# Segment 0 loads its successor's left rows through an idle buffer, turns the second left values ahead of the softmax weights, and the MLP's first loads come in another order

## The chip, the cores and the metric

One core of one Trainium2 chip. The metric is the device time of one execution in microseconds (us). A core has a matrix engine (TensorE, "PE" in the profile, with its weight loads as "PEld"), a vector engine (VectorE, "DVE"), a scalar engine (ScalarE, "ACT"), a general one (GpSimd, "POOL") and a sequencer for transfers (SyncE, "SP"). Loads and stores are issued on the queues of SP, ScalarE or GpSimd, and the same DMA engines carry them out.

## The reference

The output is `x + A(layernorm(x)) + B(layernorm(x))` for 2048 rows of 1024 bf16 numbers. B is an MLP with a hidden width of 3584. A is attention with a recurrent memory: the rows come in 64 segments of 32, and the first 8 output rows of a segment are the memory of the next.

```python
xn = _layernorm(x, axis=-1)
return x + _A_ref(xn, ...) + _B_ref(xn, ...)

# A, for each of 64 segments
h = concatenate([mem, xs])          # 8 + 32 rows
q, k, v = h @ Wq, h @ Wk, h @ Wv    # 32 heads of 128
p = softmax(where(mask, q @ k.T * scale, -1e9))
o = (p @ v) @ Wo
mem = o[:8]; outs.append(o[8:])

# B
h = gelu(x @ w1 + b1)
return h @ w2 + b2
```

## The kernel before

The program has two stages. The first is the MLP, with the layer norm (profile: up to about 401 us). The second goes through the 64 segments one after the other, since each needs the memory of the one before it.

**The MLP's start.** `load_x` (L386) brings tiles of 128 rows of x, `load_w1` (L397) a pair of column blocks of `w1`, all on SP's queue, in the order x0, x1, w1 pair 0, x2, x3, w1 pair 1, `b1rows` (L404), w1 pairs 2 to 5. While the first x is on its way, TensorE does `WARM` = 13 products on the identity (`idle_products`, L563). Then for each x tile: VectorE's statistics (L438, L440), ScalarE's square root (L447), VectorE's reciprocal and normalization (L453, L457), eight transposes on TensorE (L466), and ScalarE copies the result out (L471). Between the tiles TensorE begins the first MLP products: `begin(tt, pair)` multiplies x tile `tt` with w1 pair `pair` (two groups of eight products, L550). `BEGIN_AT` says which of them run after which transposes. VectorE does these steps in the order written, so the first statistics of tile 2 (`ln_half(tt + 2, 0)` at the end of the turn of tile 0) stand ahead of the normalization of tile 1.

**A segment.** 24 of its 32 rows and the 8 memory rows are the 32 columns of `hT`, its main rows. The other 8 rows of four segments in a row are put together, 32 columns again, as the group's left rows, `hrL` (`hL` in the code). `renew_left` (L317) copies a part of them into `hrL` from a buffer that `load_left_rows` (L313) has filled. The weights are 64 units of 512 KB: for K, Q and V two half-passes of eight units each, in the order K0, Q0, K1, Q1, V0, V1, and 16 units for O. 47 units stay in the core's memory. 17 are streamed anew for each segment, into a ring of six places (L299, SP's queue); two of these come from copies kept in PSUM (L284, VectorE). A place takes its next load when the product that used it is done (`unit_done`).

`half_pass` goes through the eight units of a half-pass: products with the main rows (L856, `hr_home`) and, where the group needs them, with the left rows (L856, `hrL`). Segment 0 does all six half-passes for the left rows of group 0, three units behind the main ones. Functions placed in `at` run between the units: `scores`, `exps`, `sums` and `values` are the attention steps. `sums(u)` makes the softmax denominators, and at its end the weights `pd` (L1024 and L1028 on VectorE). `values(u, ...)` multiplies them with the values: L1043 for the main rows, L1049 for the left rows. The left values of a half-pass, `VL[u]`, are copied out of PSUM (L914) into a staging buffer and turned by `by_slot` with two transposes on VectorE (L920, L921). In segment 0 the staging buffer of V1 is `hr_home`, the 512 columns of both `homes`.

`homes[0]` and `homes[1]` are the two halves of `hr_home`. `homes[s % 2]` holds the main rows of segment s; `load_x_rows(s + 1)` (L309) fills the other one with the next segment's rows, and L1191 then loads the residual into the one that is free again. In the first seven segments these loads are issued by ScalarE (`loads`), and `renew_left` runs on VectorE (`mover`).

After V1 come the O units (L1093). Unit 5 is followed by `values(1, ...)`. Ahead of unit 12 `fold` (L1108 on ScalarE, L1109 and L1110 on VectorE) and at the end L1227 put the four blocks of the sums together. Then, at the end of segment 0:

```python
lead_products(LEAD_FIRST)                        # 16 products on hrL, for segment 1's V0
put_mem(o_sb, nxt["hT"], mixed[:, 224:288], ...) # L344 on TensorE, L354 on VectorE, into homes[1]
lead_products(LEAD)                              # 8 more
```

and segment 1's products on `hr_home` begin. In the kernel before, the left rows of group 1 for two segments are loaded at O unit 6 of segment 0, into `pd_main`, and copied at once:

```python
if n == 6 and first:
    load_left_rows(1, 0, 2, pd_main[:, 0:128], loads)
    renew_left(pd_main[:, 0:128], 0, 2, mover)
```

The order on each engine and queue is the order in which the program writes the instructions; no planner moves them.

Of the kernel before, what the change touches and what calls it, by code (L numbers as in the profile page):

```python
# [17 lines left out]
P = 128  # L18
# [45 lines left out]
LATER = 4  # L64
LAG = 3
STREAM_BUFS = 6
WARM = 13
FILL = 4
LATE_FROM = 5
BEGIN_AT = ((), (), ((0, 1), (1, 1)), ((2, 1),))  # L70
BEGUN = 4
NPAIR = 12
MAIN_FIRST = True
# [54 lines left out]
def kernel(  # L128
# [16 lines left out]
    nc = tc.nc  # L145
# [163 lines left out]
        eng.dma_start(out=homes[s % 2], in_=rows_d[s, :, :])  # L309
        nxt["hT"] = homes[s % 2].rearrange("p (k t) -> p k t", k=KT)  # L310

    def load_left_rows(g, s0, s1, out, eng=nc.sync):
        eng.dma_start(out=out, in_=rowsL_d[g, :, 64 * s0:64 * s1])  # L313

    def renew_left(rows, s0, s1, eng):

# [56 lines left out]
    with tc.tile_pool(name="ma", bufs=2) as ma:  # L373
# [7 lines left out]
        def load_x(tt):  # L381
            k = tt // 2 % 4
            if tt % 2 == 0:
                pairs_of_x[k] = slab(f"xt{k}")
            xt = pairs_of_x[k][:, DM * (tt % 2):DM * (tt % 2) + DM]
            nc.sync.dma_start(out=xt, in_=x_flat[tt * P:(tt + 1) * P, :])  # L386
            return xt

        xtoks = {tt: load_x(tt) for tt in range(2)}
        o_sb = nat_home  # L390
        nc.vector.memset(o_sb[:, 0:8, :], 0.0)
        w1_sb, w2_sb = [], []
# [6 lines left out]

        b1rows = ma.tile([FC, P], BF16, name="b1rows", bufs=1)  # L400
        load_w1(range(1))
        xtoks.update({tt: load_x(tt) for tt in range(2, 4)})
        load_w1(range(1, 2))
        nc.sync.dma_start(out=b1rows[:, :], in_=B_b1.rearrange("(fc p) -> fc p", p=P))  # L404
        load_w1(range(2, 6))
        masks_out()
        for j in range(4):
# [153 lines left out]
        def idle_products(n):  # L561
            for _ in range(n):
                nc.tensor.matmul(  # L563
                    idle.rearrange("p (a b) -> p a b", b=P), lhsT=ident, rhs=ident[:, None, :].to_broadcast([P, 4, P]),
                    start=True, stop=True,
                )

        def begin(tt, pair):
            for k0 in range(0, KT, 4):
                for fb in (2 * pair, 2 * pair + 1):  # L570
                    first_product(begun[fb], fb, xnT, 4 * tt, 4 * tt + 4, range(k0, k0 + 4))
# [5 lines left out]
        for tt in range(4):  # L577
            ln_rstd(tt, tt + 1)
            pT = turned(ln_apply(tt))
            for t, pair in BEGIN_AT[tt]:  # L580
                begin(t, pair)
            if tt == 0:
                idle_products(FILL)
            if tt < 3:
                ln_half(tt + 1, 1)
            turned_out(tt, pT, 0, xnT, nc.scalar.copy if tt < 3 else nc.vector.tensor_copy)
            if tt < 3:
                ln_sqrt(tt + 1, tt + 2)
            turned_out(tt, pT, 1, xnT, nc.scalar.copy)
            begin(tt, 0)  # L590
            if tt < 2:
                ln_half(tt + 2, 0)
# [10 lines left out]
        for tg in range(4):  # L603
# [19 lines left out]
            for fb in range(FC):  # L623
                if tg == 0 and fb < BEGUN:
                    ps = begun[fb]
# [129 lines left out]
    with tc.tile_pool(name="late", bufs=1) as late:  # L755
# [70 lines left out]
        for s in range(NSEG):  # L826
# [103 lines left out]
            def turn_k(ps, u):  # L930
                st["kT", u] = nat_home
                turn(ps, nat_home, nc.scalar.copy)
# [64 lines left out]
            def sums(u):  # L997
                prA, prB = st["pr", u]
                dA = mixed[:, 0:160].rearrange("p (c q) -> p c q", q=40)
                for j in range(4):  # L1000
                    q = slice(32 * j, 32 * j + 32)
                    nc.tensor.matmul(
                        dA[q, :, :], lhsT=bd[:, j:j + 1].to_broadcast([P, 32]), rhs=prA, start=True, stop=False,
                        skip_group_check=True, tile_position=(0, 32 * j),
                    )
                for j in range(4):
                    q = slice(32 * j, 32 * j + 32)
                    nc.tensor.matmul(
                        ends(dA[q, :, :]), lhsT=bd[:, j:j + 1].to_broadcast([P, 32]),
                        rhs=prB,  # L1010
                        start=False, stop=True, skip_group_check=True, tile_position=(0, 32 * j),
                    )
                nc.scalar.activation(out=mixed[:, 0:160], in_=mixed[:, 0:160], func=ACT.Ln)  # L1013

                for b in (1, 0):
                    nc.scalar.activation(  # L1016
                        out=mixed[:, 160 * b:160 * b + 160], in_=mixed[:, 0:160], func=ACT.Exp, scale=-1.0,
                        bias=off[:, b:b + 1],
                    )
                pdA = pd_main.rearrange("p (c b q) -> p c b q", c=4, b=2)  # L1020
                place = qL_slots[0] if first or VALUES_0[i4][0] < VALUES_0[i4][1] else ko_slots[0]
                pdB = q_all[:, 512:640] if u else place[:, :, i4]
                dd = mixed[:, 0:320].rearrange("p (b c q) -> p b c q", b=2, q=40)
                nc.vector.tensor_tensor(  # L1024
                    out=pdA.rearrange("p c b q -> p b c q"), in0=prA[:, None, :, :].to_broadcast([P, 2, 4, 40]),
                    in1=dd, op=ALU.mult,
                )
                nc.vector.tensor_tensor(  # L1028
                    out=pdB.rearrange("p (c b a q) -> p b c a q", c=4, b=2, q=NL),
                    in0=prB[:, None, :, :, :].to_broadcast([P, 2, 4, 2, NL]),  # L1030
                    in1=dd.rearrange("p b c (e q) -> p b c e q", q=NL)[:, :, :, ::4, :], op=ALU.mult,
                )
                st["pd", u] = pdA, pdB
# [90 lines left out]
                lambda ps: turn_kL(ps, 0),  # L1124
            )
            turn_k(psK, 0)

            def first_queries(ps):

# [30 lines left out]

            def staged(u):

                return lambda ps: values_out(ps, (VL[1] if u == 0 else hr_home) if first else qL_flat[u], nc.vector.tensor_copy if u == 0 else nc.scalar.copy)

            psV, psVL = half_pass("V", 0, left_v[0], {}, staged(0))
            if first:
# [16 lines left out]

            psV1, psV1L = half_pass("V", 1, left_v[1], at)
            st["V", 1] = values_out(psV1, v_home, nc.scalar.copy)
            if left_v[1]:
                staged(1)(psV1L)
            if first:
                by_slot(1, hr_home)
                load_x_rows(s + 1, loads)  # L1190
            loads.dma_start(out=homes[s % 2], in_=res_d[s + 1, :, :])  # L1191
            if i4 == 1 and more:
# [7 lines left out]
            for n, unit in enumerate(O_UNITS):  # L1200
                t = unit_tile(unit)
                if n == NPAIR and not left_o:
                    st["folded"] = fold(psX)
                    psX = new_acc()
                o_product(n, t, psX)
                unit_done(unit)
                for fn in at.get(n, ()):
                    fn()
                if n == 6 and first:
                    load_left_rows(1, 0, 2, pd_main[:, 0:128], loads)  # L1210
                    renew_left(pd_main[:, 0:128], 0, 2, mover)
                if n == 6 and left_o:
                    st["resL"] = pd_main[:, 0:256]
                    loads.dma_start(
                        out=st["resL"], in_=resL_d[g, :, :]
                    )
# [91 lines left out]
```

## Time and profile before

| | |
|---|---|
| median of 3 runs | 1748.77 us (1744.26 to 1749.96) |
| the profiled execution | 1745.82 us, its span 1744.1 us |
| TensorE busy | 97% of the span |
| VectorE, ScalarE, GpSimd busy | 60%, 40%, 16% |
| MLP, about | 0 to 401 us |
| segment 0, about | 401 to 437 us |
| a later segment, about | 20.8 us ((1740 - 431) / 63) |
| read from HBM, written | 558.98 MB, 26.54 MB |

How to read it: times in a row are microseconds from the start of the span. A row of the order in time has start, length, engine, line, operation, output and inputs, and how many instructions were merged; in brackets stands the idle time ahead of it and what ended it. `ACTq` and `SPq` are the issues of transfers by ScalarE and SP; a transfer lands later than its issue ends. A row of the waits has the waiting engine and line, what it waited for, the sum, the number of times and the longest. A row of a stretch has its bounds, its length, the busy time of PE, PEld, DVE, ACT and POOL (with instructions), the clock that TensorE was granted (1.00 is full), the share of time that the DMA engines were busy, and GB/s. The DMA share can pass 1, since packets overlap.

### The profile page before, as it was taken

The page shows a single profiled execution, that of the slowest core. Times are in us where ns is not written, and L with a number is a line of the kernel's source. Part 1 is how long each engine was busy: PE and PEld are TensorE (multiplying, and loading weights), DVE is VectorE, ACT ScalarE, POOL GpSimd, SP SyncE. Part 2 cuts the span into 40 slices and gives each one's busy share as a digit, 9 for nine tenths or more (in the row PEclk, how much of TensorE's full clock was granted, in tenths as well). Part 3 has the DMA queues.
Part 4 walks back from the last instruction along what each step waited for, and adds up shares of the span by engine and source line. Part 5 has one row for each costly group of instructions (what it writes and reads, how often), then busy time and mean ns, then how long its engine had stood idle before and what let it go on. Part 6 is the DMA issues. An engine that isn't in the chain of part 4 may idle for free. (4 is left out here: it accounts for less than half of the span.)

```text
span 1744.1 us, 66334 instructions
## 1 busy us (share of the span) xinstructions
PE 1688.5 (97%) x28348; PEld 835.4 (48%) x28368; DVE 1040.6 (60%) x2656; ACT 702.5 (40%) x1743; POOL 287.2 (16%) x575
## 2 busy tenths in 40 slices
PE   9999999998999999999999999999999999999998
PEld 5444444444444444544444544444444444444444
DVE  7648383844555565656565565656565656565655
ACT  6335160612333334444443344444434444344433
POOL 0000001412210112121211121111212121212111
PEclk9999999999999999999999999999999999999999
DMA  9446321879999999999999999999999999999998
GB/s 278 155 147 190 84 56 41 269 257 355 336 374 376 369 391 370 399 385 397 376 401 379 394 383 389 391 380 398 380 401 382 395 375 386 367 396 382 398 382 323
DMA packets 236635, 579.36 MB, mean 332 GB/s; under 512 B 63747, under 2 KB 92611, under 8 KB 236340
## 3 DMA queue, kind: packets, MB, share of 16 engines
q1 hardware_dynamic: 204120, 555.50, 84.8%
q0 software_dynamic: 15680, 14.35, 2.5%
q10 hardware_dynamic: 16540, 5.28, 1.2%
q8 instruction: 222, 3.64, 0.8%
q14 instruction: 73, 0.60, 0.1%
HBM read 558.98 MB, written 26.54 MB: 336 GB/s over the span
## 5 line engine op out<-in xcount | busy, mean ns | idle before, releaser
L856 PE MATMUL acc<-u,hr_home 128*32 128x512 bf16 x11456 | 760.9, 380 | 13.5 <-DMA u<-Wc_V 5.3
L856 PEld LDWEIGHTS <-hr_home 128*32 128x32 bf16 x12288 | 333.9, 97 | 313.3 <-issue 40.7
L856 PE MATMUL acc<-u,hrL 128*32 128x512 bf16 x2991 | 259.4, 382 | 5.8 <-DVE hrL L317 5.6
L550 PE MATMUL ps<-u 128*128 128x512 bf16 (+1 forms) x992 | 195.4, 358 | 0.8 <-ACT u L471 0.7
L910 ACT CAST d_oL<-acc 128x512 bf16<-128x512 f32 x143 | 82.8, 583 | 253.0 <-PE acc L856 197.9
L284 DVE TENSOR_SCALAR u<-kept 128x512 uint32<-128x512 uint32 x254 | 162.0, 679 | 30.0 <-PE acc L856 21.7
L1093 PE MATMUL acc<-u,d_oL 128*32 128x512 bf16 x2560 | 162.1, 380 | 1.8 <-DMA u<-Wc_O 1.6
L1093 PE MATMUL acc<-u,kq 128*32 128x256 bf16 (+1 forms) x2688 | 137.9, 319 | 12.5 <-DMA u<-Wc_O 10.6
L681 PE MATMUL ps<-u 128*128 128x512 bf16 x657 | 145.2, 379 | 0.8
L550 PEld LDWEIGHTS <-u 128*128 128x128 bf16 x992 | 91.8, 98 | 102.9 <-issue 1.1
L1093 PEld LDWEIGHTS <-kq 128*32 128x32 bf16 x3328 | 86.9, 96 | 92.3 <-issue 23.7
L1024 DVE TENSOR_TENSOR pd_main<-kq,mixed 128x320 bf16<-128x320 bf16 x128 | 62.4, 488 | 112.0 <-ACT mixed L1016 110.1
L1270 POOL DMA_DIRECT2D out_dram<-hr_home x168 | 85.0, 512 | 251.0 <-DVE hr_home L1246 250.6
L940 ACT CAST kq<-acc 128x256 bf16<-128x256 f32 x256 | 88.9, 375 | 89.2 <-PE acc L856 52.5
L993 DVE TENSOR_TENSOR kq<-kq,mixed 128x96 bf16<-128x96 bf16 x128 | 26.1, 204 | 163.0 <-ACT kq L986 84.0
L856 PEld LDWEIGHTS <-hrL 128*32 128x32 bf16 x3200 | 85.7, 97 | 58.2 <-issue 6.4
L944 DVE STREAM_TRANSPOSE kq<-kq 128x256 bf16<-128x256 bf16 x256 | 98.0, 421 | 16.9 <-ACT kq L940 16.8
L914 ACT CAST kq<-acc 128x512 bf16<-128x512 f32 x128 | 75.1, 587 | 80.0 <-PE mixed L975 77.7
L681 PEld LDWEIGHTS <-u 128*128 128x128 bf16 x672 | 65.6, 98 | 78.8 <-DVE u L638 0.4
L630 ACT ACTIVATE u<-ps,b1col 128x512 bf16<-128x512 f32 x112 | 76.5, 684 | 66.2 <-PE ps L550 64.2
L1016 ACT ACTIVATE mixed<-mixed,small_consts 128x160 f32<-128x160 f32 x256 | 94.3, 368 | 8.4
L1093 PEld LDWEIGHTS <-d_oL 128*32 128x32 bf16 x2560 | 65.1, 96 | 57.1 <-issue 3.0
(142 smaller groups left out, 1912.7 us busy)
## 6 DMA issues: line engine op xcount, KB each, us to landing
u<-Wc_K SPq DMA_DIRECT2D x256, 512.0 KB
u<-Wc_O SPq DMA_DIRECT2D x256, 512.0 KB
u<-Wc_Q SPq DMA_DIRECT2D x192, 512.0 KB
u<-Wc_V SPq DMA_DIRECT2D x192, 512.0 KB
u<-Wc_V SPq DMA_DIRECT2D x63, 320.0 KB
u<-in_B_w_dram SPq DMA_DIRECT2D x28, 512.0 KB
u<-in_A_Wq_dram SPq DMA_DIRECT2D x13, 512.0 KB
u<-in_A_Wv_dram SPq DMA_DIRECT2D x12, 512.0 KB
```

The source lines that it names most:

```text
L284: nc.vector.tensor_single_scalar(out=out, in_=in_, scalar=0, op=ALU.bitwise_or)
L550: nc.tensor.matmul(ps[:, SEG * s0:SEG * s1].rearrange("p (s t) -> p s t", t=SEG), lhsT=w1_sb[fb // 2][:, kt, (fb % 2) * P:(fb % 2 + 1) * P ...
L630: nc.scalar.activation(out=xb[:, :], in_=ps[:, :], func=ACT.Identity, bias=b1col[:, fb:fb + 1], scale=1.0)
L681: nc.tensor.matmul(ps[:, :], lhsT=gts[fc // 4][:, fc % 4, t * P:(t + 1) * P], rhs=w2_sb[fc // 2][:, fc % 2, cs], start=(fc == 0), stop=(fc ...
L856: nc.tensor.matmul(o, lhsT=lhs[:, i, :], rhs=m, start=(i == seq[0]), stop=(i == seq[-1]), tile_position=(0, 32 * j),)
L910: cp(out=out, in_=ps.rearrange("p (h e) -> p h e", e=32))
L914: cp(out=t[:, :], in_=ps[:, :])
L940: nc.scalar.copy(out=q_home[:, h0:h1, NL:40], in_=ps[:, 32 * h0:32 * h1].rearrange("p (h e) -> p h e", e=32))
L944: nc.vector.transpose(out=half, in_=half)
L1016: nc.scalar.activation(out=mixed[:, 160 * b:160 * b + 160], in_=mixed[:, 0:160], func=ACT.Exp, scale=-1.0, bias=off[:, b:b + 1],)
L1093: nc.tensor.matmul(acc[r0:r0 + rows, 0:256 * len(blocks)], lhsT=lhsT, skip_group_check=True, rhs=o_columns(t, k, blocks), start=start, sto ...
L1270: loads.dma_start(out=out_flat[rows, 256 * j:256 * j + 256], in_=res[32 * j:32 * j + NX, :])
```

## The change

1. The left rows of group 1 for two segments are loaded right after K0 of segment 0, by SP, into `homes[1]`, which holds nothing between the MLP and segment 1's rows. They are copied into `hrL` right after V1, ahead of the copy of the second left values.
2. In segment 0 the second left values are copied out by VectorE, no longer by ScalarE, and turned before the weights of the second half are made: these are split from `sums` as `weights(u)`, and in segment 0 `weights(1)` follows `by_slot(1, ...)`.
3. At the MLP's start x2 is loaded ahead of w1 pair 0, `b1rows` goes to ScalarE's queue, `WARM` is 12, and `begin(tt - 1, 1)` runs after the transposes of each tile from the second on.

```diff
-WARM = 13
+WARM = 12
-BEGIN_AT = ((), (), ((0, 1), (1, 1)), ((2, 1),))
...
-    def load_left_rows(g, s0, s1, out, eng=nc.sync):
-        eng.dma_start(out=out, in_=rowsL_d[g, :, 64 * s0:64 * s1])
+    def load_left_rows(g, s0, s1, out):
+        nc.sync.dma_start(out=out, in_=rowsL_d[g, :, 64 * s0:64 * s1])
...
-        xtoks = {tt: load_x(tt) for tt in range(2)}
+        xtoks = {tt: load_x(tt) for tt in range(3)}
...
         load_w1(range(1))
-        xtoks.update({tt: load_x(tt) for tt in range(2, 4)})
+        xtoks[3] = load_x(3)
         load_w1(range(1, 2))
-        nc.sync.dma_start(out=b1rows[:, :], in_=B_b1.rearrange("(fc p) -> fc p", p=P))
+        nc.scalar.dma_start(out=b1rows[:, :], in_=B_b1.rearrange("(fc p) -> fc p", p=P))
...
             pT = turned(ln_apply(tt))
-            for t, pair in BEGIN_AT[tt]:
-                begin(t, pair)
             if tt == 0:
                 idle_products(FILL)
+            else:
+                begin(tt - 1, 1)
...
+                if not (first and u):
+                    weights(u)
+
+            def weights(u):
+                prA, prB = st["pr", u]
                 pdA = pd_main.rearrange("p (c b q) -> p c b q", c=4, b=2)
...
             turn_k(psK, 0)
+            if first:
+                load_left_rows(1, 0, 2, homes[1][:, 0:128])
...
-                return lambda ps: values_out(ps, (VL[1] if u == 0 else hr_home) if first else qL_flat[u], nc.vector.tensor_copy if u == 0 else nc.scalar.copy)
+                return lambda ps: values_out(ps, (VL[1] if u == 0 else hr_home) if first else qL_flat[u], nc.vector.tensor_copy if first or u == 0 else nc.scalar.copy)
...
             st["V", 1] = values_out(psV1, v_home, nc.scalar.copy)
+            if first:
+                renew_left(homes[1][:, 0:128], 0, 2, mover)
             if left_v[1]:
                 staged(1)(psV1L)
             if first:
                 by_slot(1, hr_home)
+                weights(1)
                 load_x_rows(s + 1, loads)
...
-                if n == 6 and first:
-                    load_left_rows(1, 0, 2, pd_main[:, 0:128], loads)
-                    renew_left(pd_main[:, 0:128], 0, 2, mover)
```

## The prediction

> **What bounds the kernel now.** The page was read first, then the list of waits, then the place of the longest TensorE wait in order of time, and last the same place by stretches.
>
> ```profile
> span 1744.1 us, 66334 instructions
> PE 1688.5 (97%) x28348; PEld 835.4 (48%) x28368; DVE 1040.6 (60%) x2656; ACT 702.5 (40%) x1743; POOL 287.2 (16%) x575
> ...
> DVE hrL L317 <- DMA pd_main<-rowsL_d: 6.6, 1, 6.6
> PE acc L856 <- DVE hrL L317: 5.6, 1, 5.6
> PE acc L1093 <- DMA u<-Wc_O: 12.1, 29, 1.0
> ```
>
> TensorE is busy for 97% of the span, so a change gains where TensorE stands still. Its longest single wait stands in the rows of L317: at the end of segment 0 it waits 5.6 us for `hrL`, which VectorE can't write until 32 KB of left rows have landed. The last row is the other limit: from 440 us on, TensorE waits 29 times for a streamed weight, in all 12.1 us.
>
> In order of time (columns: start, length, engine, line, operation):
>
> ```profile
> 423.81 0.84 PE L856 MATMUL acc<-u,hrL 128*32 128x512 bf16 x12
> 425.89 0.64 PE L1043 MATMUL acc<-pd_main,kq 64*128 64x80 bf16 x8
> 427.73 0.23 PE L1049 MATMUL acc<-kq,VL 64*128 64x128 bf16 x2 [1.20 <-DVE VL L921]
> 429.03 0.61 PE L1093 MATMUL acc<-u,kq 128*32 128x512 bf16 x8 [0.53 <-ACT kq L1062]
> 429.90 1.17 PE L1093 MATMUL acc<-u,kq 128*32 128x256 bf16 x32
> 436.64 1.90 PE L856 MATMUL acc<-u,hrL 128*32 128x512 bf16 x16 [5.57 <-DVE hrL L317]
> 439.47 0.64 PE L856 MATMUL acc<-low,hr_home 128*32 128x512 bf16 x4
> 440.72 0.38 PE L856 MATMUL acc<-u,hr_home 128*32 128x512 bf16 x4
> ...
> 419.91 0.69 DVE L914 CAST VL<-acc 128x512 bf16<-128x512 f32 x1 [1.19 <-PE acc L856]
> 423.80 0.63 DVE L1062 CAST d_oL<-acc 128x256 bf16<-128x256 f32 x2 [1.06 <-PE acc L1049]
> 425.22 0.49 DVE L1024 TENSOR_TENSOR pd_main<-kq,mixed 128x320 bf16<-128x320 bf16 x1 [0.80 <-ACT mixed L1016]
> 425.75 0.29 DVE L1028 TENSOR_TENSOR kq<-kq,mixed 128x128 bf16<-128x128 bf16 x1
> 426.96 0.71 DVE L921 STREAM_TRANSPOSE VL<-hr_home 128x512 bf16<-128x512 bf16 x1
> 436.36 0.23 DVE L317 COPY hrL<-pd_main 128x128 bf16<-128x128 bf16 x1 [6.58 <-DMA pd_main<-rowsL_d]
> 438.75 0.23 DVE L354 CAST hr_home<-mixed 128x64 bf16<-128x64 f32 x1 [0.72 <-PE mixed L344]
> ...
> 425.59 0.59 ACT L914 CAST hr_home<-acc 128x512 bf16<-128x512 f32 x1
> 427.75 0.33 ACTq L309 DMA_DIRECT2D hr_home<-rows_d  x1
> 428.12 0.45 ACTq L1191 DMA_DIRECT2D hr_home<-res_d  x1
> 428.61 0.37 ACT L1062 CAST kq<-acc 128x256 bf16<-128x256 f32 x1 [2.42 <-PE acc L1093]
> 428.71 0.34 ACTq L313 DMA_DIRECT2D pd_main<-rowsL_d  x1
> ```
>
> The O products end at 429.90 + 1.17 = 431.07; the next product starts at 436.64. The load was issued at 428.71 and used at 436.36, 7.65 us later. After the wait TensorE is slow as well: the 16 products on `hrL` take 1.90, though 12 took 0.84 before it. The same place by stretches (length, TensorE busy, ..., granted clock, DMA share, GB/s):
>
> ```profile
> 431.00:436.60 5.60, 0.08 (x4) 0.00 (x0) 0.23 (x1) 0.00 (x0) 1.65 (x3) 0.75 1.03 396
> 436.60:442.00 5.40, 5.36 (x62) 1.97 (x66) 2.53 (x7) 0.00 (x0) 1.65 (x3) 0.62 0.28 75
> 442.00:446.00 4.00, 4.00 (x96) 2.03 (x92) 2.43 (x8) 1.80 (x5) 2.18 (x4) 1.00 0.82 288
> 446.00:476.00 30.00, 28.73 (x590) 14.73 (x582) 18.23 (x49) 13.96 (x39) 7.17 (x13) 1.00 1.02 380
> ```
>
> TensorE's stop also stops the DMA engines, a little later: they are full until 436.6, then at 0.28 and 0.82, because the weight places stay occupied, and full again (1.02) from 446.
>
> **Part by part.** *The left rows' load* (`load_left_rows(1, 0, 2, ...)`) goes from ScalarE's queue, after O unit 6, to SP's queue right after the first K half-pass, at about 407 us, into `homes[1]`. Even at its 7.65 us it lands by 415; `hrL` may be overwritten only when its last product of segment 0 ends, 423.81 + 0.84 = 424.65. It has some 10 us of cover. On SP it takes about 0.35 us (the 0.34 of L313), and as the program's eight completion semaphores of the load queues go round, the next loads of V wait for one load later than they did. Their cover is a full DMA queue; the price is 0, and 0.35 us of DMA at the most if it is gone.
>
> *`renew_left`* now runs behind the V products: VectorE 0.23 at 424.70. *The second left values* are copied by VectorE instead of ScalarE (0.69, by the L914 row of 419.91, for 0.59) and turned before the weights: copy 424.97 to 425.66, two transposes of 0.71 to 427.15 (before: 426.96 + 0.71 = 427.67). Then the weights: L1024 to 427.68, L1028 to 428.0 (before: 426.04). So TensorE's L1043 starts at 427.75 for 425.89 and, with 0.64 and 0.23, the values end near 428.6 for 427.96: 0.65 us worse. Behind it waits ScalarE's L1062, which before was held until 428.61 by the issue of two loads (427.75 and 428.12). These now go out at 427.25, so ScalarE is free at 428.1 and L1062 follows the values at 428.65. The O products go on at about 429.1 for 429.03. I take 0 to 0.1, between 0 and 0.65; all of it lies ahead of the wait that comes next.
>
> *What is late next.* With `hrL` ready, its first 16 products (0.84 for 12 and 0.23 more, so 1.1) run from 431.1 to 432.2. The memory rows are put (L344) near 432.1, and VectorE's L354 then writes into `homes[1]`, into which segment 1's rows must have landed. When do they? SP's queue tells it:
>
> ```profile
> 431.61 9.30 SPq L299 DMA_DIRECT2D u<-Wc_Q  x2
> ...
> SPq L299 <- DMA hr_home<-rows_d: 1.4, 1, 1.4
> ...
> q1 hardware_dynamic: 408, 1.42, 101.2%
> ...
> q10 hardware_dynamic: 365, 0.14, 21.1%
> ```
>
> SP issued one load at 431.61 (some 0.3 of issue) and then waited 1.4 us for the rows' semaphore: they landed near 433.3, 5.5 us after issue. The row of q1, SP's queue, is from the queues of 427.5 to 431, where ScalarE's queue, q10, has no row: it has not moved one packet, and moves 365 in the next stretch, 431 to 433.5. It stood behind weights issued earlier. Issued 0.5 us sooner, behind the same weights, the rows land between 432.8 and 433.3; I take 433.2, as nothing is issued in those 0.5 us. L354 then ends near 433.45, and the first product on `hr_home` starts at 433.5: a new wait of about 0.9 us, too short to lower the clock (the 1.20 us before 427.73 did not: eight products in 0.61 at 429.03).
>
> [...]
>
> *TensorE's gain.* The fourth group on `hr_home`, the first at full speed, starts at 440.72; after the change at 433.5 + 3 x 0.23 = 434.2 (a group of four takes 0.38 and three groups 0.84, so (0.84 - 0.38) / 2 = 0.23 from start to start). That is 6.5 us.
>
> *The DMA's gain* is smaller, and it is what counts: in the stretch 446 to 476 the queue is full (1.02) while TensorE stands still for 1.3 us, so the weights, not TensorE, end each of the next segments. What the queue lost is 5.4 x (1.03 - 0.28) / 1.03 = 3.9 plus 4.0 x (1.03 - 0.82) / 1.03 = 0.8, together 4.7 us by shares; by bytes, 5.4 x (396 - 75) / 396 + 4.0 x (396 - 288) / 396 = 5.5. I take 5.2, nearer the bytes, since small packets raise the share; ends 4.7 and 6.5.
>
> *The MLP's start.*
>
> ```profile
> 1.43 5.73 PE L563 MATMUL ps<-hr_home 128*128 128x512 bf16 x13 [1.43 <-POOL hr_home masks.py:199]
> 8.38 1.25 PE L550 MATMUL ps<-u 128*128 128x128 bf16 x16
> 10.22 0.62 PE L466 MATMUL pT<-hr_home,u 128*128 128x128 bf16 x8 [0.59 <-DVE u L457]
> 11.52 1.27 PE L550 MATMUL ps<-u 128*128 128x128 bf16 x16 [0.67 <-ACT u L471]
> ...
> 8.82 0.69 DVE L438 BATCH_NORM_STATS2 ln_stats<-u 128x6 f32<-128x512 bf16 x1 [1.68 <-DMA u<-in_A_x_dram]
> ...
> DMA packets 1401, 1.30 MB, mean 194 GB/s; under 512 B 57, under 2 KB 1005, under 8 KB 1401
> ...
> DMA packets 2585, 2.06 MB, mean 231 GB/s; under 512 B 114, under 2 KB 2073, under 8 KB 2585
> ```
>
> One idle product less is 0.43 (5.73 over 13 and a tail), and the third x tile ahead of the first weights frees VectorE's 1.68 us wait, so the second transposes (10.22) could start 0.4 to 1 us sooner. Against this, the first weights move back by 256 KB (0.7 us at about 350 GB/s): the products at 8.38 start between 7.95 and 8.9. Then `begin(0, 1)` now stands ahead of `begin(1, 0)` and needs the second weights, which keep their place in the queue: packets 128 x 4 + 1024 x 2 = 2560. The packet counts are those up to 6.7 and to 8.9 us. Packet 1408, the end of the third tile, passed at 6.7, and VectorE had the tile at 8.82, a lag of 2.1; packet 2560 passed by 8.9, so the second weights land near 11.1. From there the same seven groups of products and two transposes remain as from 11.52 before. I take -0.3 us; ends -1.9 (no wait, 9.6) and +0.7 (the weights later by the first ones' 0.7). `b1rows` on ScalarE's queue costs one issue (some 0.4 us) ahead of the first table load, which is wanted long after; 0.
>
> *Sum:* -5.2 - 0.3 = -5.5 us, from 1745.82 (1.7 more than its span) to 1740.3. The profiled execution is 3.0 under the median of the runs (1748.77), the four executions' middle is 1747.3; on that level the forecast is 1741.8.
>
> **The rivals.** (B) The whole stall goes: the rows land before L354 (the other queue's packets let by), and segment 1 has slack in its streams. L354 then ends near 432.6, the fourth group on `hr_home` starts at 432.65 + 0.69 = 433.35, and TensorE gains 440.72 - 433.35 = 7.4, with the MLP 7.7: 1739.6. For it: TensorE's own gain is above the DMA's; against it: the DMA share of 1.02. (C) Only part is kept: the queue's 3.9 us, and the second weights land 0.7 late: -3.2, 1744.1. For it: the share is already 1.03 when TensorE would go on. (D) Slower: TensorE now enters segment 1 with its weights just landing, and each of the 63 segments ends in a short wait for `Wc_O`; it would need 5.5 / 63 = 0.09 us a segment more than today to cancel the gain, and 0.17 to be 0.3% slower: 1752.5. For it: 29 such waits stand there already. Against it: the order of instructions from segment 1 on is the same. (E) The change doesn't do what it says: the left rows land after 431, on SP behind weights; 16 us at 7.65 us a load exclude it nearly.
>
> **How the numbers follow.** 0.3% is 5.2 us, about what a measurement of this kernel can tell from no change. Chances: forecast 0.55, B 0.20, C 0.16, D 0.07, E 0.02. The forecast's own range is 5.0 to 6.8 with the MLP (1740.5 to 1742.3), three quarters of it over 5.2; with B that makes 0.62 faster. The last quarter, C and E are 0.31 within. D is slower. The range of 1738 to 1747 leaves out D and the tails: it takes in B and C and the 1.5 us by which runs stand off their middle.
>
> **What would show it.** Right: no wait for `hrL` in the list; a wait of 0.5 to 1.2 us at L354 for `rows_d`; the granted clock full from 424 to 450; DMA share above 1 all through; the first product on `hr_home` near 433.2 (433.5 less the MLP's 0.3); one wait for the second weights near 11 us. Wrong: TensorE waiting over 2 us at segment 1's V or O products, which would be C, or the rows landing before 432, which is B, or the waits for `Wc_O` after 500 us well over today's, which is D.

## The result and the profile after

The changed kernel takes 1740.31 us (median of 17 runs, 1734.42 to 1744.04), the kernel before 1747.30 (17 runs): a ratio of 0.9958, with a 95% interval of 0.9945 to 0.9970. By that ratio it is 7.3 us less, between 5.2 and 9.6. The profiled execution took 1743.2 us with a span of 1741.5; it lies on the upper side of its runs, while that of before lay on the lower side, so the two spans differ by only 2.6 us. The places compared below are near the start of the attention stage. Segment 0 does not start at the same time in every run, so the table below counts them from its start, the first product on `hr_home`.

TensorE's waits of the changed kernel between 420 and 480 us:

```profile
PE acc L1097 <- DMA u<-Wc_O: 2.8, 4, 1.3
PE acc L1047 <- DVE pd_main L1028: 1.6, 1, 1.6
PE acc L855 <- DMA u<-Wc_V: 1.2, 1, 1.2
```

The wait for `hrL`, 5.6 us before, is gone. In its place stand waits for streamed weights (`Wc_O`, `Wc_V`), and one for the weights of the second half (`pd_main`), which are now made later. The changed kernel in order of time (L855 answers to L856 of before, L1097 to L1093, L1047 to L1043, L353 to L354):

```profile
400.92 0.40 PE L855 MATMUL acc<-u,hr_home 128*32 128x512 bf16 x4
427.16 0.32 PE L1047 MATMUL acc<-pd_main,kq 64*128 64x80 bf16 x8 [1.61 <-DVE pd_main L1028]
430.33 0.84 PE L1097 MATMUL acc<-u,kq 128*32 128x256 bf16 x24 [0.86 <-DMA u<-Wc_O]
430.99 1.05 PE L855 MATMUL acc<-u,hrL 128*32 128x512 bf16 x16
432.12 0.61 PE L855 MATMUL acc<-u,hrL 128*32 128x512 bf16 x8
432.80 0.40 PE L855 MATMUL acc<-low,hr_home 128*32 128x512 bf16 x4
433.46 0.39 PE L855 MATMUL acc<-u,hr_home 128*32 128x512 bf16 x4
```

In the kernel before, segment 0 starts 0.85 us later:

```profile
401.77 0.40 PE L856 MATMUL acc<-u,hr_home 128*32 128x512 bf16 x4
```

VectorE's two copies of memory rows, of segment 0 and of segment 1:

```profile
432.52 0.23 DVE L353 CAST hr_home<-mixed 128x64 bf16<-128x64 f32 x1 [0.87 <-DMA hr_home<-rows_d]
454.08 0.23 DVE L353 CAST hr_home<-mixed 128x64 bf16<-128x64 f32 x1 [0.31 <-DMA VL<-rowsL_d]
```

The products on `hrL` follow the O products at once. VectorE waits 0.87 us for segment 1's rows, but TensorE still has eight products on `hrL` to do, and starts on `hr_home` 432.80 - 432.12 = 0.68 after their start. In a run told below in which the rows were there in time (9 groups more) the same step takes 0.44. So TensorE loses about 0.24. The fourth group on `hr_home` starts at 433.46, against 440.72. The copy one segment later is at 454.08; in the kernel before it stands here:

```profile
459.28 0.22 DVE L354 CAST hr_home<-mixed 128x64 bf16<-128x64 f32 x1 [0.52 <-DMA hr_home<-res_d]
```

So TensorE is 7.26 us sooner at the first place and 5.20 at the second. Of both, 0.85 was there at the start of segment 0 (400.92 for 401.77); counted from that start, the gains are 6.41 and 4.35. By stretches (columns as before):

```profile
431.00:436.60 5.60, 5.41 (x98) 2.30 (x88) 2.14 (x5) 0.60 (x2) 1.49 (x3) 1.00 1.03 394
436.60:442.00 5.40, 5.33 (x118) 2.95 (x121) 3.42 (x10) 2.74 (x8) 1.70 (x5) 1.00 0.99 336
442.00:446.00 4.00, 2.76 (x70) 1.36 (x62) 2.16 (x7) 1.37 (x4) 1.63 (x3) 1.00 1.00 368
446.00:476.00 30.00, 27.77 (x556) 14.34 (x558) 18.04 (x48) 11.86 (x33) 7.15 (x13) 1.00 1.01 382
```

In these stretches the clock is full and the DMA share does not fall under 0.99. Now it is TensorE that stands still from 442 to 446 (2.76 of 4.00), for a streamed weight.

### The profile page after: what moved, and what is told of

Read it like the earlier page. It is cut to its first block, busy times and chain, and to the rows that moved or that the text cites. A ratio compares the mean times of both kernels' runs of the same rounds, so it can differ in the third digit from the quotient of the medians.

```text
span 1741.5 us, 66351 instructions
## 1 busy us (share of the span) xinstructions
PE 1685.8 (97%) x28367; PEld 837.6 (48%) x28367; DVE 1040.8 (60%) x2657; ACT 702.1 (40%) x1742; POOL 287.2 (16%) x575
## 5 line engine op out<-in xcount | busy, mean ns | idle before, releaser
L855 PE MATMUL acc<-u,hr_home 128*32 128x512 bf16 x11456 | 760.1, 380 | 16.4 <-DMA u<-Wc_V 7.4
L855 PEld LDWEIGHTS <-hr_home 128*32 128x32 bf16 x12288 | 336.3, 97 | 314.1 <-issue 41.1
L855 PE MATMUL acc<-u,hrL 128*32 128x512 bf16 x2991 | 257.8, 380 | 0.0
L1097 PE MATMUL acc<-u,d_oL 128*32 128x512 bf16 x2560 | 161.8, 380 | 5.7 <-DMA u<-Wc_O 5.3
L1097 PE MATMUL acc<-u,kq 128*32 128x256 bf16 (+1 forms) x2688 | 137.0, 319 | 14.4 <-DMA u<-Wc_O 12.8
L1097 PEld LDWEIGHTS <-kq 128*32 128x32 bf16 x3328 | 87.2, 96 | 92.0 <-issue 24.3
L855 PEld LDWEIGHTS <-hrL 128*32 128x32 bf16 x3200 | 85.8, 97 | 49.8 <-issue 4.2
L1097 PEld LDWEIGHTS <-d_oL 128*32 128x32 bf16 x2560 | 65.5, 96 | 61.0 <-issue 6.5
```

The source lines that it names most:

```text
L855: nc.tensor.matmul(o, lhsT=lhs[:, i, :], rhs=m, start=(i == seq[0]), stop=(i == seq[-1]), tile_position=(0, 32 * j),)
L1097: nc.tensor.matmul(acc[r0:r0 + rows, 0:256 * len(blocks)], lhsT=lhsT, skip_group_check=True, rhs=o_columns(t, k, blocks), start=start, sto ...
```

## The experiments

Theory: from segment 1 on, the streams of weights end each segment. What the stall cost is the time for which the DMA queue ran dry, some 5 us, and TensorE has 1 to 2 us to spare. Rivals: TensorE's own length counts in full; the order of values and weights carries part of the gain; the MLP carries it.

**The left rows alone** (the kernel before with part 1 of the change):

```diff
...
             turn_k(psK, 0)
+            if first:
+                load_left_rows(1, 0, 2, homes[1][:, 0:128])
...
             st["V", 1] = values_out(psV1, v_home, nc.scalar.copy)
+            if first:
+                renew_left(homes[1][:, 0:128], 0, 2, mover)
...
-                if n == 6 and first:
-                    load_left_rows(1, 0, 2, pd_main[:, 0:128], loads)
-                    renew_left(pd_main[:, 0:128], 0, 2, mover)
```

> The kernel before with the left rows' part alone: loaded by SP behind the first K half-pass into the idle home and moved by VectorE behind the V products; the second left values are still copied by ScalarE and turned behind the weights, and the MLP starts as before. Theory (the wait for the left rows is the whole of segment 0's gain, and the weight streams let 5.2 us of it through): no wait for hrL; the segment's rows, issued near 427.7 as before, land near 433.2, so VectorE waits for them at the memory rows and TensorE's first product on hr_home stands near 433.5; the clock stays full; segment 1's memory-row copy at 454.1 (459.28 before), and the time is 5 to 6 us under before. Rival 1 (the order of values and weights carries part of it): the copy stands 1 us or more later than 454.9, the gain is 4 us or less. Rival 2 (all of TensorE's gain counts): copy at 452.0, gain 7 us.

Measured: 0.9970 (0.9959 to 0.9982), 5.2 us under before; the copy at 453.04. Counted from segment 0's start, the copy came at 52.36; the forecast, 454.1 less 401.77, was 52.33. This part alone brings segment 1's gain, and the first rival falls. The second (all of TensorE's gain counts) is not tested by this run, since TensorE gained only 4.96 at the fourth group; the runs with more work below decide it. The reason is something that was not expected: a halved clock, by which TensorE came to the memory rows so late that VectorE did not wait for segment 1's rows. Three stretches of this run, in order of time:

```profile
424.00:429.75 5.75, 3.29 (x62) 1.30 (x56) 4.05 (x9) 2.24 (x6) 1.65 (x3) 1.00 1.04 408
429.75:433.16 3.41, 3.41 (x56) 1.94 (x48) 1.30 (x4) 0.37 (x1) 1.65 (x3) 0.50 1.04 395
433.16:436.00 2.84, 2.84 (x58) 1.29 (x54) 1.32 (x4) 0.00 (x0) 0.00 (x0) 1.00 0.99 378
```

After 5.75 us in which TensorE was busy for 3.29, with no single wait over 1.20, the clock was halved for 3.41 us. The last section shows what such stretches have in common.

**All but the left rows' early load** (the changed kernel, with the load and its copy back at O unit 6):

```diff
...
-            if first:
-                load_left_rows(1, 0, 2, homes[1][:, 0:128])
...
-            if first:
-                renew_left(homes[1][:, 0:128], 0, 2, mover)
...
+                if n == 6 and first:
+                    load_left_rows(1, 0, 2, pd_main[:, 0:128], loads)
+                    renew_left(pd_main[:, 0:128], 0, 2, mover)
```

> The changed kernel with the left rows' load put back to where it was (ScalarE's queue, behind O unit 6, into pd_main, moved by VectorE there); the second left values are still turned ahead of the weights and the MLP starts in the new order. Theory (the early load is what ends the wait): the load is issued near 428.1, lands 7 us later, TensorE waits 4 to 5.5 us for hrL and comes to it near 435.5; the halved clock, the DMA queue's low share and segment 1's memory-row copy near 458.5 (before 459.28, changed 454.08) come back, and the time is that of the MLP part alone, 1 to 2 us under before. Rival (turning the left values first, by which the loads are issued sooner, is enough by itself): wait under 2 us, copy under 456.

```profile
435.02 1.90 PE L855 MATMUL acc<-u,hrL 128*32 128x512 bf16 x16 [4.89 <-DVE hrL L316]
```

The stall is back, 4.89 us long, with the slow products behind it; the copy is at 458.81 and the time at 0.9989 (0.9974 to 1.0005), 1.9 us under before. The early load is what ends the wait; the new order alone only shortens it.

**The weights ahead again** (the changed kernel):

```diff
-                if not (first and u):
-                    weights(u)
+                weights(u)
...
                 by_slot(1, hr_home)
-                weights(1)
```

> The changed kernel with the weights ahead again: they are worked out as soon as the sums are there, and the second left values are turned behind them (VectorE still copies them). Theory (the order moves work about in front of a limit that lies elsewhere): TensorE's values products start near 425.6 without the 1.61 us wait, the rows are issued 0.7 us later, land near 433.1, and the first product on hr_home stands 0.5 to 0.7 us later than 432.80; segment 1's memory-row copy stays within 0.4 us of 454.08, the time within 1 us of the changed kernel's. Rival (TensorE sets segment 1's end): that copy is 0.5 to 0.7 us later. Rival (the order costs more than it gives, as the 1.61 us wait suggests): the O products end 1 us sooner, the rows are not late, and the copy is 1 us sooner.

TensorE's first values products start at 425.15, and the first product on `hr_home` at 433.73, counted from segment 0's start 1.5 us later than in the changed kernel. The copy is at 453.53. The time is 0.9970 (0.9957 to 0.9984), 2.1 us over the changed kernel's where within 1 was forecast, but the two intervals overlap. So the new order is worth up to 1.5 us on TensorE in segment 0, and nothing that can be seen one segment later. Most of the 1.5 can be a halved clock, as in the left rows' run: it was halved from 428.37 to 431.78, with TensorE busy for 2.88 of it, which at full clock is an estimated 1.4 us less. The O products did not end sooner (at 432.27, 1.7 later than in the changed kernel from segment 0's start), so the second rival falls.

**More work for TensorE.** 9, 18, 26 and 34 groups of products on `hrL` were put ahead of those that count. They write where the first true product writes next, so nothing of the computation changes.

```diff
                 led.update(next=(w, u, new_acc(), ahead, order), made=0)
+                if first:
+                    for _ in range(18):   # 9, 18, 26, 34
+                        product(w, ahead[0], u, res_tiles[w, ahead[0], u], hL, led["next"][2], ahead[:1], True)
                 lead_products(LEAD_FIRST)
```

> The changed kernel with nine more groups of four products on hrL at the end of segment 0, ahead of the first that counts (9 x 0.215 = 1.9 us of TensorE; they are overwritten). Theory (from segment 1 on the weight streams end each segment, and 2.1 us of TensorE's 7.26 are slack): the fourth group on hr_home at 433.46 + 1.9 - 0.8 (the wait for the rows is covered) up to + 1.9, that is 434.6 to 435.4; segment 1's memory-row copy within 0.5 us of 454.08; the waits for streamed weights in segment 1 shrink from 5 us to about 3. Rival (TensorE's own length counts): the copy at 455.2 to 456.0, and the time 1.1 to 1.9 us over the changed kernel's.

> The same with eighteen groups (3.9 us). Theory: TensorE's fourth group on hr_home near 437.2; 2.1 us are slack, so segment 1's copy stands 1.5 to 2.0 us later, near 455.8; the DMA queue falls under its share somewhere in 434 to 442. Rival (TensorE's length counts): 458.0. Rival (the slack is larger than 2.1, and the 5.2 of the result was chance): within 0.5 us of 454.08.

> The changed kernel with 26 more groups on hrL at segment 0's end (5.6 us, overwritten), between the 18 groups that cost nothing (fourth group on hr_home 435.84, copy 454.62) and the 34 that cost 5 us (439.60, copy 458.75). Theory (TensorE has 2.1 us of slack against the streams here, and every us beyond it counts in full): fourth group near 437.7, copy at 454.1 + (437.7 - 433.46 - 2.06) = 456.3; time 2 us over the changed kernel's. Rival (a threshold further out: the queue loses nothing until all places are full): copy under 455.2. Rival (the length counts from the first us, and the earlier copies were chance): 457.8 or more.

> The same with 34 groups (7.3 us), the length of TensorE's gain: as in the kernel before TensorE comes to hr_home near 440.7, but it is busy in between and its clock stays full. Theory (what counts is how long the weight places stay occupied): DMA share under 0.5 in some stretch of 436 to 441 as before, segment 1's copy near 454.1 + 5.2 = 459.3, and the time 4.5 to 6 us over the changed kernel's, that is that of the kernel before less the 0.6 us of the MLP. Rival (the idle time and its low clock were what cost, not the occupied places): the copy at 457 or less.

The table takes all runs but three, which are told further below, in the order of the third column: the start of segment 0 (its first product on `hr_home`), the fourth group on `hr_home` in segment 1 and the copy at segment 1's end, the last two counted from the first; then the ratio of the times to before.

| kernel | start of segment 0 | fourth group | copy | ratio |
|---|---|---|---|---|
| changed | 400.92 | 32.54 | 53.16 | 0.9958 |
| rows on SP's queue | 400.83 | 33.69 | 53.47 | 0.9966 |
| left rows alone | 400.68 | 33.99 | 52.36 | 0.9970 |
| weights ahead | 400.35 | 34.04 | 53.18 | 0.9970 |
| 9 groups more | 400.08 | 34.52 | 52.69 | 0.9960 |
| 18 more | 400.06 | 35.78 | 54.56 | 0.9954 |
| 26 more | 401.29 | 37.39 | 56.29 | 0.9975 |
| without the early load | 400.22 | 38.91 | 58.59 | 0.9989 |
| before | 401.77 | 38.95 | 57.51 | |
| 34 more | 399.41 | 40.19 | 59.34 | 0.9992 |

Up to 34.5 us, the copy does not move with the fourth group: 52.97 is the mean of the first five rows, which lie between 52.36 and 53.47. From 35.8 on it comes 18.6 to 19.7 us after the fourth group, 19.01 in the mean of the last five: each us of TensorE then counts in full. The two lines meet at 52.97 - 19.01 = 33.96. The changed kernel has 33.96 - 32.54 = 1.4 us to spare, and the kernel before lay 5.0 us beyond the bend; by the scatter of the rows, the bend is known to about half a microsecond. 18 groups, 3.9 us of work, moved the copy by 1.4 and the time not at all. They moved the fourth group by 3.2: the wait for the rows was covered (0.2), and the O products ended 0.4 sooner. That they would move the copy by 1.5 to 2.0 was nearly right; the fourth group came at 435.84, not at 437.2. With 26 groups it came at 438.68, a microsecond later than forecast, and so did the copy (457.58 for 456.3, where the rival had 457.8 or more). Counted from where TensorE came, 4.85 later than in the changed kernel, the theory's slack of 2.06 gives a copy at 55.95, the rival 58.01; it came at 56.29. With 9 the copy came sooner than forecast, at 452.77, which is within the scatter of the first five rows, and TensorE's waits for streamed weights between 433 and 456 us fell from 2.5 to 0.6 us. For 34 groups the same place by stretches, at full clock throughout,

```profile
431.00:436.00 5.00, 5.00 (x100) 2.80 (x96) 0.00 (x0) 0.00 (x0) 1.33 (x3) 1.00 0.86 333
436.00:441.00 5.00, 5.00 (x98) 2.44 (x90) 1.38 (x4) 0.00 (x0) 3.47 (x7) 1.00 0.16 44
```

and its copy at segment 1's end:

```profile
458.75 0.23 DVE L353 CAST hr_home<-mixed 128x64 bf16<-128x64 f32 x1 [0.58 <-PE mixed L343]
```

TensorE is busy without a pause, and yet the DMA share falls to 0.16 and the time of before is nearly back (0.9992, 0.9976 to 1.0008). SP's waits for TensorE, between 429 and 446 us, in the kernel before, with 34 groups and in the changed kernel:

```profile
SPq L299 <- PE acc L856: 10.0, 5, 7.3
SPq L298 <- PE acc L855: 8.4, 5, 5.7
SPq L298 <- PE acc L855: 2.4, 6, 0.6
```

These are the waits of the weight loads for a place that TensorE's products still hold. It was not the idle engine or its clock that cost, but that the weight places stayed occupied. The table reaches to the end of segment 1; for the later segments only the times of whole runs speak.

**More work for the DMA queue.** Three O weights that are in memory are read once more into their places at segment 1's start; the computation is unchanged.

```diff
             st = {}
+            if s == 1:
+                for unit in [v for v in O_UNITS if not IS_STREAMED[v]][-3:]:
+                    fetch(res_tiles[unit], unit)
```

> The changed kernel with three useless weight loads (O weights that are there already, read once more from memory into the same places: 3 x 512 KB) on SP's queue at the start of segment 1; TensorE's work is unchanged. At 395 GB/s they are 4.0 us of the queue, as much as the 18 groups were of TensorE. Theory (the weight streams end segment 1): the copy stands 3.5 to 4.5 us later, near 458, with as much more waiting for streamed weights on TensorE, and the time is 3 to 4.5 us over the changed kernel's. Rival (TensorE ends it, or the queue has room): copy within 1 us of 454.08, time within 1 us.

```profile
PE acc L858 <- DMA u<-Wc_Q: 3.9, 1, 3.9
PE acc L1100 <- DMA u<-Wc_O: 0.3, 1, 0.3
```

These are TensorE's waits from 433 to 456 us, and this is the copy at segment 1's end:

```profile
458.55 0.23 DVE L353 CAST hr_home<-mixed 128x64 bf16<-128x64 f32 x1 [0.43 <-DMA VL<-rowsL_d]
```

TensorE came to segment 1 as early as in the other kernels (fourth group at 33.15) and then waited 3.9 us for one weight; the copy came 57.12 us after segment 0's start, 4.0 later than the changed kernel's 53.16. Behind this wait the clock was halved from 446.36 to 449.77, but that is not what ended the segment, since TensorE waited for streamed weights again later:

```profile
455.44 0.40 PE L1100 MATMUL acc<-u,kq 128*32 128x512 bf16 x4 [0.31 <-DMA u<-Wc_O]
456.88 0.62 PE L1100 MATMUL acc<-u,kq 128*32 128x256 bf16 x16 [0.17 <-DMA u<-Wc_O]
```

The slower clock can be a reason, which no run tested, why the waits grew less than forecast: 4.2 us between 433 and 456 us for 2.5 in the changed kernel, where 3.5 to 4.5 more was expected. The time, 0.9990 (0.9974 to 1.0005), is 5.6 us over the changed kernel's by the two ratios, over the 3 to 4.5 of the forecast; each ratio is known to some 2 to 3 us. About 4 us of work moved the copy by 1.4 on TensorE and by all of their length on the queue. That is what the theory says, and the rival falls.

**Segment 1's rows on SP's queue** (the changed kernel):

```diff
-                load_x_rows(s + 1, loads)
+                load_x_rows(s + 1)
```

> The changed kernel with segment 1's rows issued by SP's queue, the weights' own, instead of ScalarE's. They are asked for at the same place, but SP may be held by its wait for a free weight place. Theory (a load stands behind what was issued before it, whichever queue it is on): rows issued at the same time land within 0.5 us of 432.5; if SP issues them x us later they land x later. [...]

```profile
426.99 0.32 SPq L308 DMA_DIRECT2D hr_home<-rows_d  x1
427.40 0.38 SPq L298 DMA_DIRECT2D u<-Wc_Q  x1
```

SP's queue in order of time; and VectorE's copy into the rows:

```profile
433.58 0.22 DVE L353 CAST hr_home<-mixed 128x64 bf16<-128x64 f32 x1 [1.95 <-DMA hr_home<-rows_d]
```

The rows were issued 0.22 us later than in the changed kernel (426.99 for 426.77) and used 1.06 later, though one load of 512 KB, issued ahead of them there, is behind them here. The sixteen completion events that each load has in the traces show how:

```
                     queue    issued   first done  last done
changed   Wc_Q       SP       425.59   431.92      434.53
          rows       ScalarE  426.77   432.12      432.43
rows on   Wc_K       SP       424.29   430.26      433.31
SP        rows       SP       426.99   430.88      433.49
          residual   ScalarE  426.99   431.06      432.61
```

By the first event, the rows came behind the weights issued just ahead of them: 0.20 us behind with the rows on ScalarE's queue (432.12 for 431.92), 0.62 with the rows on SP's (430.88 for 430.26). By the last, the load on ScalarE's queue was complete ahead of SP's weights (432.43 for 434.53), and the load on SP's was not (433.49 for 433.31). So the theory holds by the first event and not by the last. The rows were used 0.09 us after their last event in both runs, and so ScalarE's queue was the better one, by 1.06 - 0.22 = 0.84 us in this pair of executions. It is no rule: in the kernel before, the 32 KB of left rows on ScalarE's queue had their first event at 432.76 and the last at 436.34, later than weights that SP issued 0.8 us after them (435.98). For the time nothing came of it (copy 53.47): the rows are not what ends segment 1.

**The MLP's part alone** (the kernel before with part 3 of the change; its core):

```diff
-WARM = 13
+WARM = 12
...
-        xtoks = {tt: load_x(tt) for tt in range(2)}
+        xtoks = {tt: load_x(tt) for tt in range(3)}
...
-            for t, pair in BEGIN_AT[tt]:
-                begin(t, pair)
...
+            else:
+                begin(tt - 1, 1)
```

> The kernel before with the MLP's part alone: third x tile ahead of the first weights, b1rows on ScalarE's queue, twelve idle products instead of thirteen, the second pair of products begun one tile later. Theory: the first group of the main loop starts at 18.5 instead of 19.09, one wait for the second weights near 10.9, and everything later is earlier by the same 0.6 us; time 0.6 us under before, which the interval of whole runs will hardly tell from nothing. Rival (the -0.3 of the forecast was right, and the rest of what the two profiles differ by is chance): 18.8. Rival (the later first weights cost more later on): segment 0 starts no earlier than 401.8.

**The fourth x tile behind the second weights** (the changed kernel):

```diff
-        load_w1(range(1))
-        xtoks[3] = load_x(3)
-        load_w1(range(1, 2))
+        load_w1(range(2))
+        xtoks[3] = load_x(3)
```

> The changed kernel with the fourth x tile loaded behind the second weights instead of ahead of them. Theory (the second weights end the wait at 10.94, and 256 KB at about 350 GB/s are 0.7 us): that wait of 0.93 us shrinks to 0.2 or 0.3, the main loop starts at 17.8 to 18.0 instead of 18.47, the time is 0.5 us under the changed kernel's. Rival (the fourth tile is late next): VectorE waits for it, its transposes come as much later, and the main loop starts at 18.4 to 18.8.

The MLP's part alone takes 0.9986 (0.9972 to 1.0000), 2.4 us under before. Its main loop starts at 17.56, not 18.5: this moment varies from run to run. In the ten profiles with the new order and the loads as changed it lies between 17.20 and 18.47, at 17.88 in the mean; in the two with the old order it is 19.09 and 18.46. The gain is about 0.9 us, as far as two old profiles tell. At the start of segment 0 it is about 0.7 (400.5 in the mean of the ten, 401.2 of the two), and the rival that had segment 0 start no earlier than 401.8 falls (400.51). In each of the ten the main loop starts 7.53 or 7.54 us after the first product on the second weights, so it is their arrival that varies. With the fourth tile behind, the wait for them shrinks from 0.93 to 0.26, but VectorE then waits for that tile, and these 7.53 us become 7.91. So the rival's mechanism is there, though not its size: the main loop starts at 17.71, among the others, and not at 18.4 to 18.8.

TensorE's and VectorE's row of the run with the fourth tile behind:

```profile
9.80 1.96 PE L548 MATMUL ps<-u 128*128 128x128 bf16 x32 [0.26 <-DMA u<-in_B_w_dram]
```

```profile
10.49 0.70 DVE L436 BATCH_NORM_STATS2 ln_stats<-u 128x6 f32<-128x512 bf16 x1 [1.03 <-DMA u<-in_A_x_dram]
```

Its time of 0.9954 (0.9937 to 0.9972) cannot be told from the changed kernel's. The profiles of this run and of the MLP's part alone are left out of the table, since in both the clock was halved for 3.41 us inside segment 1, behind waits of 1.91 and 1.73 us for `Wc_O`; their copies come at 61.83 and 55.86, 2 to 3 us later than the bend would have them.

## Why the prediction was right, point by point

- *The wait for `hrL`* goes: right, by the left rows' part alone and not without it. The copy into `hrL` starts at 424.29 behind the last product that reads the old rows, with no wait for the load, so rival E falls.
- *The new wait for the rows*: forecast 0.9 us on TensorE, up to a first product on `hr_home` at 433.5, which is 31.73 us after segment 0's start. The product came at 31.88, and VectorE's wait was 0.87. But TensorE lost only about 0.24 to it. The wait of 1.61 for the weights of the second half was in the forecast: the O products were to go on 27.33 us after segment 0's start (429.1) and did at 27.29. What it left out is the wait of 0.86 for `Wc_O` behind that. By it the products on `hrL` started 0.74 later than forecast (30.07 for 29.33) and covered most of the rows' wait. So the time of the first product is right, and the share of the two waits in it is not.
- *That the rows stand behind SP's weights*: right by the first completion event (432.12, behind the weights' 431.92), wrong by the last (432.43, ahead of the weights' 434.53).
- *Values and weights in the new order*, 0 to 0.65 worse: the values' last product ends at 427.48 + 0.23, 26.79 after the start of segment 0, 0.6 later than before (26.19). It went into the wait for the rows, as the forecast had it.
- *TensorE's gain*, 6.5: from 38.95 to 32.54 is 6.41. Right.
- *The DMA's gain, which is the one that counts*, 5.2 between 4.7 and 6.5: between the copies 57.51 - 53.16 = 4.35 in the two profiles, 4.5 against the mean of five, 5.0 by the bend, and 5.2 (3.1 to 7.2) by the times of the left rows alone. The mechanism is shown. That small packets raise the share, as the forecast had it, is in the trace of before: from 431 to 433.5 us, q1's 206 packets moved 0.77 MB for a share of 77.0%, and q10's 365 moved 0.14 MB for 21.1%, about half as much again for the same bytes. Yet the size by shares, 4.7, was nearer to the traces than the one by bytes; by the pair of profiles the gain lies under the forecast's lower end, about as near to C's 3.9 as to that end.
- *The MLP's start*, -0.3: this is the mis-sized term. The wait for the second weights was where the forecast had it, and ended at 10.94 in the changed kernel's profile, near the 11.1; but in nine more profiles it ended at 9.67 to 10.61. The 11.1 had been read off one tile of one execution. The gain is 0.6 in this pair and about 0.9 over all profiles.
- *Sum*: -5.5 was forecast. The terms as measured, 4.5 and 0.9, make 5.4; the times say 7.3, between 5.2 and 9.6. The sum lies in that interval near its end. By times, the left rows alone (5.2) and the MLP's part alone (2.4) make 7.6, with 2 us and more either way on each. What is between 5.4 and 7.3 no trace shows, and it may be chance.
- *Rival B*, the whole stall goes: TensorE's end of segment 0 went its way (it lost about 0.24 to the rows), but segment 1 took 2 us of it back, as the queue bounds it. Its 1739.6 is within what was measured, for another reason: the MLP gave more. That the rows land before L354 because the other queue's packets are let by was a supposition that no trace of before shows: in the changed kernel ScalarE's load was complete 2.10 us ahead of SP's weights (432.43 for 434.53), and VectorE still waited 0.87 for it. *C*, part kept, falls: the second weights were sooner, not later, and its 3.2 us lie under the interval. Yet the sign that was set for it came: TensorE waited 1.24 + 1.31 = 2.55 us at segment 1's V and O products, where over 2 was to mean C. The forecast itself gives 2.2 there, since it lets TensorE gain 1.3 us more than the queue and the kernel before already waits 0.9; so this sign could not tell the two apart. *D*, drift by waits for `Wc_O` after 500 us: they add up to 15.3 us in the changed kernel's profile and 10.1 in that of before, which looked like it; but in nine further profiles with the early load they come to 5.6 to 11.6. D's sign came too, then, in one profile of ten: it is taken for chance.
- *The clock* was full, as forecast, but this was luck in part, and the reason given (a wait of 1.2 us is too short) doesn't hold in general: it was halved in the left rows' run behind the same wait of 1.20 with two others (0.74 and 0.52), and in two runs with the changed kernel's code at this place.

## What to carry to other kernels

Where one engine waits once and a queue of streamed loads is full on both sides of it, price the stall by the time that the queue runs dry and not by the engine's wait: here 6.4 us of TensorE were worth about 4.5, read at the end of one segment. Test it from both sides, by the same length of work put on the engine and on the queue; the bend between "costs nothing" and "counts in full" then gives the slack. And for a product that waits for its operand, count first what else that engine has left to do.

## What the runs showed of the hardware that was not expected

The halved clock came in stretches of 3.41 us (6.83 in three of the runs), and it followed waits of under 2 us: 1.73 and 1.91 for a single one, and three of 0.74, 1.20 and 0.52 together. The same code ran through the same waits at full clock in other runs: 1.61 and 0.86 in the changed kernel. The traces show what goes with the difference. In all thirteen, the clock changes lie whole multiples of 3.413 us apart: 426.666, 6.827 and 1303.891 us in the kernel before are 125, 2 and 382 times 3.4133, and 1733.971 in the changed kernel is 508 times. These are windows of that length in the run of the left rows alone, in the changed kernel, and in the run with the fourth tile behind:

```profile
426.33:429.75 3.42, 1.70 (x33) 0.68 (x36) 3.03 (x6) 0.58 (x2) 1.09 (x3) 1.00 1.04 413
423.80:427.21 3.41, 1.79 (x38) 0.69 (x30) 3.00 (x8) 1.42 (x4) 1.65 (x3) 1.00 1.04 402
424.43:427.84 3.41, 1.79 (x34) 0.66 (x26) 2.90 (x7) 0.92 (x3) 0.10 (x1) 1.00 1.04 403
```

The clock of the next window was halved after the first and the third, and stayed full after the second. Between 30 and 1725 us the thirteen traces have 6441 such windows at full clock. In 9 of them TensorE was busy for half of the window or less, and each was followed by a halved one. In another 9 it was busy for 0.51 to 0.53, and three of these were followed by a halved one. Of the 6423 above that, none was. So in these traces it is the busy share of one window that goes with the fall, and the same wait can fall into one window or be split between two. The changed kernel's segment 0 stands right at this border (1.79 of 3.41, 0.52). The shares rest on ends of products that the profile models, and no run was made to test the reading.

A load of 64 KB on ScalarE's queue, beside SP's full one, was not quicker by its first completion event (0.2 us behind the weights issued 1.2 us ahead of it), but its sixteen events lay within 0.31 us, where those of the weights took 2.6. The 64 KB of residual right behind it on the same queue took 1.55 (432.36 to 433.91), and the left rows of the kernel before 3.58. How far the events of one load drift apart decided here when it could be used, and what sets the drift was not tried.
